# Block minima taken from PSUM, one-element reductions as moves, and rescaling on GpSimd in a fused attention and gated-MLP kernel

## The chip, the core and the metric

The kernel runs on one core of a Trainium2 chip. The metric is device time in microseconds (us) of one execution. The engines are named as in the profile: PE (TensorE matmul), PEld (its weight loads), DVE (VectorE), ACT (ScalarE), POOL (GpSimd) and SP (SyncE, which here only issues DMAs).

## What is computed

The input x is 2048 tokens by 448 features. One branch is multi-head attention with 16 heads of 28 features, the other a gated MLP with 1792 hidden features; a sigmoid gate per token mixes them. Everything is float32.

```python
q, k, v = split(x @ wqkv)                       # 16 heads, head size 28
p = softmax(einsum("bhqd,bhkd->bhqk", q, k) * 28 ** -0.5)
a = einsum("bhqk,bhkd->bhqd", p, v) @ wo
h = relu(x @ W_gate) * (x @ W_up)
b = h @ W_down
g = sigmoid((x * gate_w).sum(-1))
out = g * a + (1 - g) * b
```

## The kernel before

The schedule is written out by hand: each engine executes its instructions strictly in the order in which the program text issues them, and waits at semaphores.

**Three stages.** First the projections (q, k, v, split into high and low float32r parts), then the attention, then the down projection with the output projection. The attention goes through 32 *visits*, two for each head `h`: visit `v` handles half of the keys (8 chunks of 128) of head `v // 2` against all queries (4 blocks `j` of 512). The gate and up projections of the MLP are threaded through the visits as filling for PE (`gu_mm`, letter `x`).

**Scores.** `score()` makes a *pair*: two 128x512 matmuls into one two-bank PSUM tile from `ps_w`, then one ACT instruction over 128x1024. The softmax maximum is found in two ways. For query blocks 0 and 1 the maximum was found one head ahead by `smax` (matmuls into another `ps_w` tile, then a DVE maximum over 128x1024, L196), and travels in two additional rows of Q, so ACT takes the exponential straight from PSUM (L290). Blocks 3 and 2 are *raw* in nearly every visit (`RAW`; visit 0 has block 3 alone): ACT copies the negated score to SBUF (L292). `block_min` then takes the minimum over the four pairs of a block on DVE (L242 for the first two pairs, L244 for the third and fourth), `all_max` brings it across partitions (a transposing reduction L255, four small moves L257, L258, L260, L261, a reduction L259, a transpose L263), `take_max` subtracts it on GpSimd, 128x2048 at a time (L269), and `take_exp` takes the exponential on ACT (L276).

**PSUM.** While the visits run, `ps_w` hands out three two-bank slots strictly in turn, to scores and to `smax` alike. The matmuls of a pair therefore wait until the pair three before it has been read by whoever reads it last. The two other banks (`ps_x`) serve the gate and up projections and the products with V.

**End of a visit.** `pv` multiplies with V, in two halves (letters P and Q, 64 matmuls in all). In odd visits `rescale` brings raw blocks of the two visits to a common maximum: part 0 (letter c) subtracts two small 32x16 pieces (L611) and transposes them (L612), part 1 (letter f) takes an exponential (L615) and multiplies the 64x512 part of the output (L616), all on DVE but the exponential. `row_sums` and `spread` send the sums through DRAM, `normalise` multiplies on GpSimd (L654).

**What sets the order.** One string per kind of visit (`FIRST`, `O4`, `E3`, `O3`, `L5` to `L7`), one letter per step: s a score pair, m a `smax`, x one gate or up matmul, b a `block_min`, A an `all_max`, g a subtraction, e an exponential, c and f the rescaling, n `smax_end`, w a weight split, P and Q the products. Scores run four pairs ahead of their visit (`AHEAD = 4`). `small_things(2 * v + 1)` runs at the tenth s of a visit.

Of the kernel before, what the change touches and what calls it, by code (L numbers as in the profile page):

```python
# [8 lines left out]
F32 = mybir.dt.float32  # L9
# [9 lines left out]
P = 128  # L19
# [23 lines left out]

NP = 10

FIRST = "sbsbxbAxxxxlusgxsxsxsxxssxsesxxxsxbxbxgsxbAxxxxxxexPwQ"

O4 = "nssxxmxsxxbsxssbxbxsxxmAxsgxxgxswxxsxsxxsxxsxsecmxxmxxxxsxbxsxmxbxxxxgmxxexxebmxxxAgxmwefPQ"

E3 = "ssxmxsxxsxsxsxsbxbxbsxAxxxgxssxsgexxmxgxxmxxxsmxxsxxsmsxeexmbxxbgexmsxmPwbAQ"  # L50

O3 = "sxsxxsmssbxbbssxxxxsmsAgxxsxsxsxxsgxxmxxemxxxxsmnscxxsbbbgxmxxxxgwxxeAexexmwmPfQ"

L5 = "ssxsbsxxsxwssxxxxbxxssxxxxssxxsxxsbxxxAsxsbxxggxbxwexsxxxxcxxbgxxxegxxxxexxxxeAnPfQ"

L6 = "sssxxxsssxbxbxxxswxxxxssssxbxxxsxxxgegsAxsgxxexxxbxxxsxbxsbxxxxxxxxgAxxxxxxPeeQ"

L7 = "ssxxxxsbbswxbxxxxxxxxxxxxsxxsxxsAxsxxxxxgxsxgxexscgxexxxfxxxegxxxexsxsxPwQ"

ROUNDS = [  # L60
    (FIRST, 2), (O4, 4), (E3, 3), (O3, 3), (E3, 3), (O4, 4), (E3, 3), (O3, 3),
# [17 lines left out]
def gated_mix_kernel(ctx, tc, x, wq, wo, wgu, wd, out):  # L79
# [40 lines left out]
    def low(dst, src, high):  # L120
        nc.vector.tensor_tensor(dst, src, f32(high), op=OP.subtract)  # L121
# [36 lines left out]
    def load_k(h):  # L158
        for r in range(4):
            nc.sync.dma_start(f32(K[h % 3])[DH * r:DH * (r + 1)], qk_d[r % 2, 2 * DH * h:2 * DH * h + DH, :])  # L160
# [39 lines left out]
    def smax_end(h):  # L200

        pt = ps_x(f"mt_{h}")
        n = NU[h]
        nc.tensor.transpose(pt[:n, :P], M.pop(h), ident)
        mr = keep.tile([n, P], F32, name=f"mr_{h}", tag="mr", bufs=1)
        mh = keep.tile([n, 2, P], F32R, name=f"mh_{h}", tag="mh", bufs=1)
        nc.scalar.activation(mr, pt[:n, :P], AF.Copy)
        nc.scalar.activation(mh[:, 0], mr, AF.Copy)
        low(mh[:, 1], mr, mh[:, 0])
        for r in range(2):  # L210
            nc.sync.dma_start(f32(Q[h])[GD + r:GD + r + 1, :n * P], f32(mh)[:, r])

# [21 lines left out]
    def block_min():  # L234

        if not todo_max:
            return
        v, j, p = todo_max[0]
        if (v, j) not in R2:
            R2[v, j] = att.tile([P, 2, TB], F32, name=f"r2_{v}_{j}", tag="r2", bufs=1)  # L240
            left[v, j] = NK // 4 - 2
            nc.vector.tensor_tensor(R2[v, j], todo_max.pop(0)[2], todo_max.pop(0)[2], op=OP.min)  # L242
            return
        nc.vector.tensor_tensor(R2[v, j], R2[v, j], todo_max.pop(0)[2], op=OP.min)  # L244
        left[v, j] -= 1
        if left[v, j]:
            return
        q = NK // 8 * (v % 2)
        todo_all.append((v, j, [(v, j, q), (v, j, q + 1)]))

    def all_max():
        v, j, quads = todo_all.pop(0)
        to = ((0, 11) if j == 2 else (9, 10))[v % 2]
        a, b = (1 - v % 2, 9) if j == 2 else (1, 9 + v % 2)
        nc.vector.tensor_reduce(MN[:, 1:3], R2.pop((v, j)).rearrange("p a (b r) -> p a b r", r=32), axis=AX.X, op=OP.min,  # L255
                                apply_transpose=True)
        nc.vector.tensor_copy(MN[:64, 3:5], MN[64:, 1:3])  # L257
        nc.vector.tensor_copy(MN[:32, 5:9], MN[32:64, 1:5])  # L258
        nc.vector.tensor_reduce(MN[:32, to], MN[:32, a:b].rearrange("p a b -> p b a"), axis=AX.X, op=OP.min)  # L259
        nc.vector.tensor_copy(MN[32:64, to], MN[:32, to])  # L260
        nc.vector.tensor_copy(MN[64:, to], MN[:64, to])  # L261
        RM[v, j] = att.tile([P, TB], F32, name=f"rm_{v}_{j}", tag="rm", bufs=2)
        nc.vector.transpose(RM[v, j], MN[:, to].unsqueeze(2).to_broadcast([P, 16, 32]))  # L263
        todo_sub.extend((v, j, q) for q in quads)
# [13 lines left out]
    def score():  # L278

        v, done, q, half, chunks = stream.pop(0)  # L280
        h = v // 2
        if q not in QUAD:
            QUAD[q] = p_slot(next(slots) % NP, f"P_{v}_{q[1]}_{q[2]}")
        ps = ps_w(f"s_{v}_{chunks[0][0]}_{chunks[0][1]}")
        for c, (k, j) in enumerate(chunks):
            nc.tensor.matmul(ps[:, c], K[h % 3][:, k * P:(k + 1) * P], Q[h][:, j * TB:(j + 1) * TB], start=True, stop=True)  # L286
            AT[v, k, j] = QUAD[q][:, 2 * half + c]
        dst = QUAD[q][:, 2 * half:2 * half + 2]
        if done:
            nc.scalar.activation(dst, ps, AF.Exp, scale=SCALE)  # L290
        else:
            nc.scalar.activation(dst, ps, AF.Copy, scale=-1.0)  # L292
            todo_max.append((v, chunks[0][1], dst))

    X = {}

# [305 lines left out]
    def rescale(v, part):  # L602

        h = v // 2
        if v % 2 == 0:
            return
        rows = slice(64, P)
        if part == 0:
            RS[h] = fe.tile([P, TB], F32, name=f"rs_{h}", tag="rb", bufs=1)
            for r, a, b in ((slice(64, 96), 11, 0), (slice(96, P), 10, 9)):  # L610
                nc.vector.tensor_tensor(MN[r, 1], MN[r, a], MN[r, b], op=OP.subtract)  # L611
            nc.vector.transpose(RS[h][rows], MN[rows, 1].unsqueeze(2).to_broadcast([64, 16, 32]))  # L612
        else:
            d = RS.pop(h)[rows]
            nc.scalar.activation(d, d, AF.Exp, scale=SCALE)  # L615
            nc.vector.tensor_tensor(OS[h][rows], OS[h][rows], d, op=OP.mult)  # L616

    PO = {}

# [46 lines left out]
    def small_things(u):  # L666

        h, q = divmod(u, 4)

        if u in (16, 32):  # L670
            g = u // 16 + 1
            nc.sync.dma_start(V[:, g % 2], v_d[g])
        if u == 1:
            gates()
        if u == 2:
            pack_wo()
        if h and q == 1:
            row_sums(h - 1)
            spread(h - 1)
            if h + 2 < H:  # L680
                load_k(h + 2)
                load_q(h + 2)

    split_f(0, act_high, pool_low, (0,))
    fetch_f(1)
    for v, (order, nu) in enumerate(ROUNDS):
# [6 lines left out]
        for o in order:  # L693
            if o == "x" and not passes:
                continue
            if o == "s":
                ns += 1
                if ns == 10:
                    small_things(2 * v + 1)
                if stream:  # L700
                    score()
            elif o == "m":
                if m < len(maxima):
                    smax(m)
                    m += 1
            elif o == "x":
                i, half, n = passes.pop(0)
                if n == 0:
                    units.append((i, half, ps_x(f"gu_{i}_{half}")))
                gu_mm(units[-1][2], i, half, n)  # L710
                if n == NT - 1:
                    i, half, ps = units.pop()
                    spill_h(i, ps) if half else relu(i, ps)
                    if half:
                        finished.add(i)
                        load_f(i + 2)
            elif o == "n":
                if v % 2 and v < 2 * H - 1:
                    smax_end(v // 2 + 1)
            elif o == "w":  # L720
                ready = nxt + (ROUNDS[v + 1][1] if v + 1 < len(ROUNDS) else 2)
                ready = min(ready + ready % 2, 2 * NF)
                while parts < ready and (parts < 4 or parts // 2 - 2 in finished):
                    split_f(parts // 2, act_high, pool_low, (parts % 2,))
                    parts += 1
                    if parts % 2 == 0:
                        fetch_f(parts // 2 + 1)
            elif o == "b":
                block_min()
            elif o == "A":  # L730
                all_max()
            elif o == "g":
                take_max()
            elif o == "e":
                take_exp()
            elif o in "cf":
                rescale(v, "cf".index(o))
            elif o == "l":
                sends.pop()()
            elif o == "u":  # L740
                split_f(0, act_high, pool_low, (1,))
                QS.append(last_q("Q2"))
                for a, b in ((GD, 12), (GD + 12, 4)):
                    nc.sync.dma_start(f32(QS[2])[a:a + b].rearrange("p j t -> p (j t)"), Q[1][GD + 2:GD + 2 + b].bitcast(F32))
                load_k(2)
                load_q(2)
                fetch_f(2)
                parts = 2
            elif o in "PQ":
                if o == "P" and v and v % 2 == 0:  # L750
                    normalise(v // 2 - 1)
                pv(v, "PQ".index(o))
        rest = [k for k in todo_exp + todo_sub + todo_all if k[0] == v]
        assert not passes and not rest and v not in PO or len(stream) == max(0, 16 * (2 * H - 1 - v) - AHEAD), (v, passes, rest, len(stream) + 16 * (v + 1))
# [184 lines left out]
```

## Time and profile before

| | |
|---|---|
| time, median of 3 runs | 1548.31 us (1546.1 to 1550.45) |
| profiled execution | 1548.23 us, span 1546.5 us |
| busy over the span | PE 1280.5 us (83%), DVE 1242.8 us (80%), ACT 875.5 us (57%), POOL 765.5 us (50%) |
| granted PE clock, mean | 0.918 |

The span is the time from the first to the last instruction of the profile; 1.73 us of the execution's own time lie around it. Busy time of DVE includes what an instruction spends being held up after it has started. PE is busy while any matmul is in its pipeline. The visits occupy about 155 to 1348 us of the span.

### The profile page before, as it was taken

To read this page: it belongs to the slowest core of one execution; us is meant where nothing else is said; L and a number is where in the kernel's file an instruction comes from. 1 tells how busy PE (TensorE), PEld (TensorE's weight loads), DVE (VectorE), ACT (ScalarE), POOL (GpSimd) and SP (SyncE) were. 2 spreads that over 40 slices of the span, in tenths; PEclk is the share of its full clock that TensorE was granted. 3 is DMA by queue.
4 is the path that set the end of the run, shared out by engine and by line. 5 is a ranking of instruction groups with operands and counts; after the bars stand their busy time and mean duration, and the time that the engine had idled before them with its cause. 6 is when DMAs were issued, how large, how long until landed. Compare 5 with 4: busy or idle time off the path is not lost. (4 is left out here: it accounts for less than half of the span.)

```text
span 1546.5 us, 16880 instructions
## 1 busy us (share of the span) xinstructions
PE 1280.5 (83%) x6183; PEld 883.9 (57%) x6183; DVE 1242.8 (80%) x1242; ACT 875.5 (57%) x956; POOL 765.5 (50%) x280
## 2 busy tenths in 40 slices
PE   9998688868787868786878788877887869779999
PEld 7886455535454535454555455545555545469998
DVE  6564889998999999899889998999788996665333
ACT  5226667766766656566665656665666766421221
POOL 4223656674755454546354635464555556454110
PEclk9999889988899989999898888999999989999999
DMA  9664433341425231413251313141514122373442
GB/s 318 232 237 162 150 103 92 112 120 64 122 89 173 59 95 64 121 52 102 90 174 52 105 60 105 60 114 51 159 64 103 54 71 76 110 233 110 133 145 79
DMA packets 63807, 178.37 MB, mean 115 GB/s; under 512 B 13498, under 2 KB 20098, under 8 KB 59074
## 3 DMA queue, kind: packets, MB, share of 16 engines
q1 hardware_dynamic: 56988, 151.00, 32.4%
q0 software_dynamic: 6304, 25.82, 4.3%
q8 instruction: 49, 0.80, 0.2%
q10 hardware_dynamic: 432, 0.46, 0.1%
q14 instruction: 34, 0.28, 0.1%
HBM read 118.58 MB, written 58.87 MB: 115 GB/s over the span
## 5 line engine op out<-in xcount | busy, mean ns | idle before, releaser
L269 POOL TENSOR_TENSOR P<-P,rm 128x2048 f32<-128x2048 f32 x102 | 484.7, 4769 | 385.4 <-DVE rm L263 323.0
L286 PE MATMUL s<-Q,K 128*128 128x512 f32 x1024 | 359.0, 445 | 177.1 <-DVE mx L196 174.7
L575 PE MATMUL gu<-X,wg 128*128 128x512 f32 x1232 | 412.9, 428 | 37.1 <-DVE h L588 21.4
L196 DVE TENSOR_REDUCE mx<-sm 128x1 f32<-128x1024 f32 x256 | 307.1, 1214 | 87.2 <-PE sm L192 86.9
L286 PEld LDWEIGHTS s<-Q,K 128*128 128x128 f32 x1024 | 203.8, 211 | 272.4 <-DVE mx L196 204.6
L575 PEld LDWEIGHTS gu<-X,wg 128*128 128x128 f32 x1232 | 257.4, 209 | 107.2 <-DVE h L588 25.7
L292 ACT ACTIVATE P<-s 128x1024 f32<-128x1024 f32 x204 | 201.2, 1025 | 196.4 <-PE s L286 195.9
L290 ACT ACTIVATE P<-s 128x1024 f32<-128x1024 f32 x206 | 201.7, 1038 | 108.6 <-PE s L286 107.7
L628 PE MATMUL po<-P,V 128*32 128x512 f32 x1640 | 235.0, 602 | 5.3 <-ACT P L276 2.8
L244 DVE TENSOR_TENSOR r<-r,P 128x1024 f32<-128x1024 f32 x102 | 197.1, 1933 | 7.3
L276 ACT ACTIVATE P<-P 128x2048 f32<-128x2048 f32 x102 | 190.7, 1908 | 12.8 <-POOL P L269 12.5
L192 PE MATMUL sm<-K,Q 128*128 128x512 f32 x520 | 174.1, 419 | 21.7 <-DVE mx L196 14.2
L269 POOL TENSOR_TENSOR V<-V,rm 128x2048 f32<-128x2048 f32 x24 | 115.6, 4817 | 90.5 <-DVE rm L263 83.2
L838 PE MATMUL acc<-WD,hh 128*128 128x448 f32 x672 | 141.0, 369 | 5.3 <-POOL WD L124 3.7
L628 PE MATMUL po<-V 128*32 128x512 f32 x408 | 137.9, 605 | 8.4 <-DVE h L588 8.4
L242 DVE TENSOR_TENSOR r<-P 128x1024 f32<-128x1024 f32 x51 | 136.8, 2683 | 7.4 <-ACT P L292 6.4
L838 PEld LDWEIGHTS acc<-WD,hh 128*128 128x128 f32 x672 | 127.4, 190 | 17.3 <-POOL WD L124 4.7
L628 PEld LDWEIGHTS po<-P,V 128*32 128x32 f32 x1640 | 63.9, 111 | 126.9 <-issue 111.4
L192 PEld LDWEIGHTS sm<-K,Q 128*128 128x128 f32 x520 | 101.7, 202 | 56.0 <-DVE mx L196 25.0
L115 ACT ACTIVATE hh<-hr 128x512 fp32r<-128x512 f32 x56 | 35.2, 631 | 127.4 <-PE acc L838 121.2
L121 DVE TENSOR_TENSOR hh<-hr,hh 128x512 fp32r<-128x512 f32 x56 | 51.2, 914 | 64.8 <-ACT hh L115 64.8
L611 DVE TENSOR_TENSOR mn<-mn 32x16 f32<-32x16 f32 x32 | 89.7, 2802 | 0.7
(86 smaller groups left out, 1264.3 us busy)
## 6 DMA issues: line engine op xcount, KB each, us to landing
wg<-ws_d SPq DMA_DIRECT2D x42, 896.0 KB
K<-qk_d SPq DMA_DIRECT2D x64, 224.0 KB
Q<-qk_d SPq DMA_DIRECT2D x64, 224.0 KB
h_d<-h SPq DMA_DIRECT2D x56, 256.0 KB
hr<-h_d SPq DMA_DIRECT2D x56, 256.0 KB
ws_d<-wg SPq DMA_DIRECT2D x14, 896.0 KB
qk_d<-st POOLq DMA_DIRECT2D x21, 512.0 KB, 3.4
wgr<-wgu SPq DMA_DIRECT2D x13, 512.0 KB
```

The source lines that it names most:

```text
L192: nc.tensor.matmul(ps[:, c, :], Q[h][:, u * P:(u + 1) * P], K[h % 3][:, k0:k0 + TB], start=True, stop=True)
L196: nc.vector.tensor_reduce(to, ps, axis=AX.XY, op=OP.max)
L242: nc.vector.tensor_tensor(R2[v, j], todo_max.pop(0)[2], todo_max.pop(0)[2], op=OP.min)
L244: nc.vector.tensor_tensor(R2[v, j], R2[v, j], todo_max.pop(0)[2], op=OP.min)
L269: nc.gpsimd.tensor_tensor(QUAD[q], QUAD[q], m, op=OP.subtract)
L276: nc.scalar.activation(q, q, AF.Exp, scale=-SCALE)
L286: nc.tensor.matmul(ps[:, c], K[h % 3][:, k * P:(k + 1) * P], Q[h][:, j * TB:(j + 1) * TB], start=True, stop=True)
L290: nc.scalar.activation(dst, ps, AF.Exp, scale=SCALE)
L292: nc.scalar.activation(dst, ps, AF.Copy, scale=-1.0)
L575: nc.tensor.matmul(ps, WS[i][:, s, a], xf(i // NF, b), start=(n == 0), stop=(n == NT - 1))
L628: nc.tensor.matmul(po[32 * j:32 * j + 32], V[:, h // 4 % 2, k, h % 4], AT.pop((v, k, j)), start=(k == k0), stop=(k == k0 + NK // 2 - 1))
L838: nc.tensor.matmul(ACC[i // NF][t][:, :D], HH[i][:, a, t * P:(t + 1) * P], WD[:, f, b], start=(f == 0 and n == 0), stop=(f == NF - 1 and n ...
```

## The change

1. In all visits but the first, `block_min` reads the newer score pair where the matmuls left it, in PSUM. It does so with a `scalar_tensor_tensor` (times -1, then minimum) whose other input is in SBUF: the negated first pair, or the running minimum. ACT still copies each raw pair to SBUF, since GpSimd works on that copy. The minimum now also holds the PSUM slot. The instruction waits for ACT's copy of the same pair.
2. The four small moves in `all_max` become `tensor_reduce` over an axis of one element.
3. Both small subtractions and the multiplication of `rescale` move from DVE to GpSimd. DVE keeps the transpose between them, which now waits for GpSimd.
4. `smax_end` reads its transposed maxima from PSUM twice, without the copy to SBUF in between (L207).
5. `normalise` gets a letter of its own, N, early in the odd visits; it stood at P of the even visits before. `small_things` comes at the sixth s; the loads of the next K and Q, which were part of it, stay at the tenth.
6. All seven order strings are written anew.

```diff
-O4 = "nssxxmxsxxbsxssbxbxsxxmAxsgxxgxswxxsxsxxsxxsxsxsecmxxmxxxxsxbxsxmxbxxxxgmxxexxebmxxxAgxmwefPQ"
...
+O4 = "ssbnxxNxxsxxxbsxbxxxsAgwxxsxgxxsssxxsxsxxxxmxexxmmxsxexgxmxxxmxsxsxmgxxmxexmsbxxsbxxscefbxPwAQ"
...
-        mr = keep.tile([n, P], F32, name=f"mr_{h}", tag="mr", bufs=1)
...
-        nc.scalar.activation(mr, pt[:n, :P], AF.Copy)
-        nc.scalar.activation(mh[:, 0], mr, AF.Copy)
-        low(mh[:, 1], mr, mh[:, 0])
+        nc.scalar.activation(mh[:, 0], pt[:n, :P], AF.Copy)
+        low(mh[:, 1], pt[:n, :P], mh[:, 0])
...
-        v, j, p = todo_max[0]
+        v, j, x, _ = todo_max.pop(0)
         if (v, j) not in R2:
-            R2[v, j] = att.tile([P, 2, TB], F32, name=f"r2_{v}_{j}", tag="r2", bufs=1)
-            left[v, j] = NK // 4 - 2
-            nc.vector.tensor_tensor(R2[v, j], todo_max.pop(0)[2], todo_max.pop(0)[2], op=OP.min)
-            return
-        nc.vector.tensor_tensor(R2[v, j], R2[v, j], todo_max.pop(0)[2], op=OP.min)
+            r = att.tile([P, 2, TB], F32, name=f"r2_{v}_{j}", tag="r2", bufs=1)
+            left[v, j] = NK // 4 - 1
+            before, (_, _, x, ps) = x, todo_max.pop(0)
+        else:
+            r = before = R2[v, j]
+            ps = _
+        R2[v, j] = r
+        if ps is None:
+            nc.vector.tensor_tensor(r, x, before, op=OP.min)
+        else:
+            nc.vector.scalar_tensor_tensor(r, ps, -1.0, before, op0=OP.mult, op1=OP.min)
         left[v, j] -= 1
...
+    def move(dst, src):
+
+        nc.vector.tensor_reduce(dst, src.unsqueeze(len(src.shape)), axis=AX.X, op=OP.min)
...
-        nc.vector.tensor_copy(MN[:64, 3:5], MN[64:, 1:3])
-        nc.vector.tensor_copy(MN[:32, 5:9], MN[32:64, 1:5])
+        move(MN[:64, 3:5], MN[64:, 1:3])
+        move(MN[:32, 5:9], MN[32:64, 1:5])
...
-        nc.vector.tensor_copy(MN[32:64, to], MN[:32, to])
-        nc.vector.tensor_copy(MN[64:, to], MN[:64, to])
+        move(MN[32:64, to], MN[:32, to])
+        move(MN[64:, to], MN[:64, to])
...
-            todo_max.append((v, chunks[0][1], dst))
+            todo_max.append((v, chunks[0][1], dst, ps if v else None))
...
-                nc.vector.tensor_tensor(MN[r, 1], MN[r, a], MN[r, b], op=OP.subtract)
+                nc.gpsimd.tensor_tensor(MN[r, 1], MN[r, a], MN[r, b], op=OP.subtract)
...
-            nc.vector.tensor_tensor(OS[h][rows], OS[h][rows], d, op=OP.mult)
+            nc.gpsimd.tensor_tensor(OS[h][rows], OS[h][rows], d, op=OP.mult)
...
-                if ns == 10:
+                if ns == 6:
                     small_things(2 * v + 1)
+                if ns == 10 and v % 2 == 0:
+                    loads(v // 2)
...
+            elif o == "N":
+                if v > 1 and v % 2:
+                    normalise(v // 2 - 1)
...
-                if o == "P" and v and v % 2 == 0:
-                    normalise(v // 2 - 1)
```

DVE in visit 19, around its rescaling, before. `h` is the hidden tile of the MLP, `mn` the small tile of minima, `rs` the rescaling factors, `mx` the maxima from a `smax` pair `sm`, `r` the running minimum and `P` a copied score in SBUF:

```order
L588 TENSOR_TENSOR h_5929<-gu_1_5874,rl_5800 128x512
L611 TENSOR_TENSOR mn<-mn 32x16 x2
L612 STREAM_TRANSPOSE rs_5983<-mn 64x512
L196 TENSOR_REDUCE mx_5877<-sm_5987 128x1
L196 TENSOR_REDUCE mx_5877<-sm_5994 128x1
L242 TENSOR_TENSOR r_20_3_6008<-P_3_0_5970 128x1024
L196 TENSOR_REDUCE mx_5877<-sm_6016 128x1
L244 TENSOR_TENSOR r_20_3_6008<-r_20_3_6008,P_3_1_6002 128x1024
```

The same engine and visit now (`s` is a score pair in PSUM):

```order
L196 TENSOR_REDUCE mx_5932<-sm_5999 128x1
L196 TENSOR_REDUCE mx_5932<-sm_6006 128x1
L248 SCALAR_TENSOR_TENSOR r_20_3_6014<-s_2_3_6010,P_3_0_5986 128x1024
L248 SCALAR_TENSOR_TENSOR r_20_3_6014<-s_4_3_6019,r_20_3_6014 128x1024
L620 STREAM_TRANSPOSE rs_6030<-mn 64x512
L248 SCALAR_TENSOR_TENSOR r_20_3_6014<-s_6_3_6026,r_20_3_6014 128x1024
L263 TENSOR_REDUCE mn<-r_20_3_6014 128x32
```

The subtractions have left DVE, the transpose has moved behind the first minima of the next visit's block 3, and those minima read `s`.

GpSimd over the same visit, before: the last two subtractions of visit 19 and the first two of visit 20 (`rm` is the maximum spread over partitions):

```order
L269 TENSOR_TENSOR P_2_2_5865<-P_2_2_5865,rm_2_5926 128x2048
L269 TENSOR_TENSOR V<-V,rm_2_5926 128x2048
L269 TENSOR_TENSOR P_3_0_5970<-P_3_0_5970,rm_3_6058 128x2048
L269 TENSOR_TENSOR P_3_1_6002<-P_3_1_6002,rm_3_6058 128x2048
```

and now the four subtractions of visit 19 and the first of visit 20, with the normalisation of the head before ahead of them:

```order
L662 TENSOR_TENSOR os_5340<-os_5340,rb_5645 128x512
L277 TENSOR_TENSOR P_3_2_5747<-P_3_2_5747,rm_3_5811 128x2048
L277 TENSOR_TENSOR P_3_3_5771<-P_3_3_5771,rm_3_5811 128x2048
L277 TENSOR_TENSOR P_2_2_5831<-P_2_2_5831,rm_2_5892 128x2048
L277 TENSOR_TENSOR V<-V,rm_2_5892 128x2048
L619 TENSOR_TENSOR mn<-mn 32x16 x2
L624 TENSOR_TENSOR os_5829<-os_5829,rs_6030 64x512
L277 TENSOR_TENSOR P_3_0_5986<-P_3_0_5986,rm_3_6064 128x2048
```

The rescaling stands between the last subtraction of one visit and the first of the next.

PE at the first raw pairs of visit 20, before (`gu` is the gate or up projection, `s_20_4_3` the pair of visit 20, key chunk 4, block 3):

```order
L286 MATMUL s_20_4_3_6003<-Q1_106,K1_103 128x512 x2
L575 MATMUL gu_32_1_5991<-X0_111,wg_32_5741 128x512 x2
L286 MATMUL s_20_6_3_6011<-Q1_106,K1_103 128x512 x2
L575 MATMUL gu_32_1_5991<-X1_112,wg_32_5741 128x512
L192 MATMUL sm_184_6016<-K2_104,Q2_1188 128x512 x2
```

and now:

```order
L192 MATMUL sm_187_6006<-K2_104,Q2_1185 128x512 x2
L294 MATMUL s_20_2_3_6010<-Q1_106,K1_103 128x512 x2
L583 MATMUL gu_33_0_5984<-X0_111,wg_33_5880 128x512 x2
L294 MATMUL s_20_4_3_6019<-Q1_106,K1_103 128x512 x2
L583 MATMUL gu_33_0_5984<-X1_112,wg_33_5880 128x512
L583 MATMUL gu_33_0_5984<-X0_111,wg_33_5880 128x512
L294 MATMUL s_20_6_3_6026<-Q1_106,K1_103 128x512 x2
L583 MATMUL gu_33_0_5984<-X1_112,wg_33_5880 128x512
```

The `smax` pairs no longer stand between these raw pairs; one or two gate or up matmuls do, and the products with V of visit 19 follow directly.

More of the change, by code (lines that the diff above doesn't have):

```diff
@@ L44 @@
 NP = 10
[L46 to L58, printed above, removed]
+FIRST = "sbsbxbAxxxlusssxxsxgsxxxxxsssxbgxexssbxxbxxxxexPwAQ"
+O4 = "ssbnxxNxxsxxxbsxbxxxsAgwxxsxgxxsssxxsxxxxmxexxmmxsxexgxmxxxmxsxsxmgxxmxexmsbxxsbxxscefbxPwAQ"
+E3 = "gsmsxbxsxbxsxxbxsxxxxsxxssxxAssxmexxmxxsxxxxmsxmgxxmexgsmxgxxmxessexsbPwbbAQ"
+O3 = "sgsxxbxxsxxxsxxbbsxxgxxAssgsxxxgsmsxmxexmxNsmnwxsmsxsmseexxbxxxxxbxxsxmexmbPcfAwQ"
+L5 = "ssNbnsxxxgxxxsxxsxbbxxsxxexxxxxsAxsxgxssxgxxsxxsxgxxxsxxsswbxxxxxwexxexexsbxcfxxPbAQ"
+L6 = "gssxsxsxxxxxbxsbxxxsbexsxxxxsxxAxxxsxsxxxsgxsxesxxsgxxbxxxxexxsgxxwxxbsbxxAxePQ"
+L7 = "gssxxgbsxwbsxxxxxsxxxexsxxbxxAsxxsxxxxxxxxxxxsxsggxxxxxxxeeexxsNxcxxxfsxwPQ"
 ROUNDS = [
@@ L679, in small_things, with loads @@
             spread(h - 1)
-            if h + 2 < H:
-                load_k(h + 2)
-                load_q(h + 2)
+    def loads(h):
+        if 2 < h + 2 < H:
+            load_k(h + 2)
+            load_q(h + 2)
     split_f(0, act_high, pool_low, (0,))
```

## The prediction

> **What bounds the kernel now.** I first cut the span into the three stages (busy time of each engine by stretch; the columns after the length are PE, PEld, DVE, ACT and POOL with instruction counts, then the granted PE clock).
>
> ```profile
> core 0: us, PE busy (x) PEld busy (x) DVE busy (x) ACT busy (x) POOL busy (x), PEclk, DMA share, GB/s
> 0.00:155.00 155.00, 148.13 (x638) 119.32 (x642) 88.50 (x110) 63.54 (x118) 50.89 (x66) 0.98 0.67 237
> 155.00:1348.00 1193.00, 945.82 (x4664) 595.43 (x4657) 1066.50 (x1025) 768.18 (x773) 663.03 (x179) 0.90 0.32 95
> 1348.00:1546.00 198.00, 186.51 (x891) 169.17 (x889) 87.83 (x109) 43.75 (x66) 51.60 (x36) 0.98 0.46 141
> ```
>
> Before and after the visits PE is busy 96% and 94% of the time, and the change hardly touches these stages. In the visits, 1193 us or 37.3 us each, PE has the larger page share, yet DVE is the fuller engine: 1066.5 of 1193 is 89%, PE 79%. The list of waits says who waits for whom:
>
> ```profile
> POOL P L269 <- DVE rm L263: 323.0, 40, 16.1
> ...
> PE s L286 <- DVE mx L196: 174.7, 48, 7.9
> ...
> PE sm L192 <- DVE mx L196: 14.2, 15, 3.3
> ```
>
> PE's largest idle time, 174.7 + 14.2 = 189 us, is waiting for a maximum on DVE to give back a PSUM slot; GpSimd too waits mostly for DVE. In the visits PE idles 1193 - 945.8 = 247 us, so 58 us have other causes.
>
> Is DVE busy with work? The views of single lines give minimum, median and maximum duration in ns:
>
> ```profile
> L242 DVE TENSOR_TENSOR r<-P x51: 1182/2964/5262, 135.5 to 1314.8; 128x1024 f32<-128x1024 f32 x51
> L244 DVE TENSOR_TENSOR r<-r,P x102: 1214/1226/5475, 136.8 to 1323.5; 128x1024 f32<-128x1024 f32 x102
> L611 DVE TENSOR_TENSOR mn<-mn x32: 166/4152/4503, 186.9 to 1332.8; 32x16 f32<-32x16 f32 x32
> L616 DVE TENSOR_TENSOR os<-os,rs x16: 689/3538/5049, 208.9 to 1338.8; 64x512 f32<-64x512 f32 x16
> L588 DVE TENSOR_TENSOR h<-gu,rl x56: 650/676/693, 164.2 to 1358.7; 128x512 f32<-128x512 f32 x56
> L196 DVE TENSOR_REDUCE mx<-sm x256: 1159/1216/1227, 54.2 to 1238.9; 128x1 f32<-128x1024 f32 x128
> L269 POOL TENSOR_TENSOR P<-P,rm x102: 4492/4612/5632, 146.7 to 1332.7; 128x2048 f32<-128x2048 f32 x102
> ```
>
> The first four take two tensors from SBUF, and all four stretch: a 32x16 subtraction that can be done in 166 ns typically takes 4152, about one GpSimd subtraction (4612). The next two, which have a PSUM input and at most one from SBUF, never stretch (693 and 1227 at most). So much of DVE's busy time is being held up by GpSimd.
>
> **The change, term by term.** DVE in the visits, for the lines L242, L244, L611, L616 and L121 in this order (us, count):
>
> ```profile
> 155.00:1348.00 1193.00, 166.47 (x62) 0.90 0.32 95
> 155.00:1348.00 1193.00, 242.03 (x124) 0.90 0.32 95
> 155.00:1348.00 1193.00, 89.68 (x32) 0.90 0.32 95
> 155.00:1348.00 1193.00, 52.57 (x16) 0.90 0.32 95
> 155.00:1348.00 1193.00, 16.64 (x15) 0.90 0.32 95
> ```
>
> *Minima.* 62 + 124 = 186 instructions, 408.5 us, become as many with one PSUM and one SBUF input. The trace has this operation in another shape:
>
> ```profile
> L844 DVE SCALAR_TENSOR_TENSOR y<-acc,gate,ga x16: 676/679/684, 1417.2 to 1542.8; 128x448 f32<-128x448 f32 x16
> ```
>
> Scaled by elements, 679 x 1024/448 = 1.55 us is the upper end; the 1.216 us maximum over the same 1024 elements (L196) is the lower. I take 1.28, nearer to L196: from L588 (512 elements, 676 ns) to L244's minimum (1024, 1214 ns) an element more costs 1.05 ns, and 679 + 576 x 1.05 = 1284 ns. 186 x 1.28 = 238 us: DVE saves 170 (bounds 120 to 182).
>
> *Rescaling.* DVE loses 89.7 + 52.6 = 142 us. GpSimd gets 32 small subtractions and 16 of 64x512; its nearest rows:
>
> ```profile
> L654 POOL TENSOR_TENSOR os<-os,rb x15: 1317/2215/2290, 234.5 to 1303.9; 128x512 f32<-128x512 f32 x15
> L124 POOL TENSOR_TENSOR wg<-wgr,wg x39: 721/1010/1995, 158.6 to 430.1; 128x384 fp32r<-128x384 f32 x26, 64x256 fp32r<-64x256 f32 x13
> ```
>
> Between nothing and 721 ns for a small one I take 0.3 (16 elements against 256 and more), and 2.0 for the others (1.3 to 2.3): 10 + 32 = 42 us, 663 + 42 = 705 on GpSimd, 22 us per visit, below PE's work. DVE's transpose now waits for GpSimd, with minima, `all_max` and hidden tiles queued behind it, and PE waits for those: see the first rival. The multiplication releases the addition to the second half's output, after 64 matmuls that PE does meanwhile.
>
> *Maxima transposed* (L121's 15):
>
> ```profile
> L121 DVE TENSOR_TENSOR mh<-mr,mh x16: 235/238/4472, 99.1 to 1277.7; 8x128 fp32r<-8x128 f32 x15, 12x128 fp32r<-12x128 f32 x1
> ```
>
> With one PSUM input instead of two SBUF inputs I take the median for all, 15 x 0.24 = 3.6 us instead of 16.6, saving 13. ACT loses 16 copies, some 4 us, hidden.
>
> *Moves.* 63 x 4, off and on in equal number:
>
> ```profile
> L257 DVE COPY mn<-mn x63: 175/177/592, 141.2 to 1326.0; 64x32 f32<-64x32 f32 x63
> L198 DVE TENSOR_REDUCE m<-mx 128x8 f32<-128x16 f32 x16 | 2.7, 170 | 0.6
> ```
>
> A reduction of 16 elements takes 170 ns, a copy 177: nothing, between -5 and +5 us. The copies hardly ever stretch here, because GpSimd is waiting for their result. The Trainium skill, SBUF — State Buffer, section "Who interferes with whom", says that a copy in a two-port mode is blocked for the whole of a GpSimd instruction, while `tensor_reduce` never contends on trn2. By that rule the moves would pay once GpSimd has work at this place, as the rescaling could give it, 16 times up to 2 us; but that would be a loss avoided, and the sum stays the same.
>
> *Normalisation, earlier small things, loads.* Same instructions, same engine. On SP's queue the loads of K stood behind the wait of `spread`:
>
> ```profile
> 924.46 0.41 SPq L644 DMA_DIRECT2D l_d<-rq  x1
> 929.09 1.71 SPq L650 DMA_DIRECT2D rb<-l_d  x4
> 930.84 1.68 SPq L160 DMA_DIRECT2D K<-qk_d  x4
> ```
>
> The 4.6 us hole moves four pairs ahead; the loads keep their place, a visit before use. Hidden; uncovered it would cost 16 x 4.6 = 74 us.
>
> *DVE's sum:* 1066 - 170 - 142 - 13 = 741 us, 23.2 per visit. It stops being the bound, so the saving is not 325 us: PE is late next.
>
> *PE's work.* Matmuls in the visits, for L286, L575, L192 and L628 (PE busy and count first):
>
> ```profile
> 155.00:1348.00 1193.00, 345.00 (x984) 195.50 (x984) 0.90 0.32 95
> 155.00:1348.00 1193.00, 395.56 (x1169) 245.39 (x1170) 0.90 0.32 95
> 155.00:1348.00 1193.00, 151.60 (x448) 88.11 (x448) 0.90 0.32 95
> 155.00:1348.00 1193.00, 234.72 (x2048) 66.81 (x2040) 0.90 0.32 95
> ```
>
> These overlap, so I price them by spacing, from the line's durations and the timeline around 900 us:
>
> ```profile
> L628 PE MATMUL po<-P,V x1640: 592/592/1062, 154.4 to 1346.9; 128*32 128x512 f32 x183
> ```
>
> ```profile
> 903.00 2.73 PE L628 MATMUL po<-P,V 128*32 128x512 f32 x20
> ...
> 909.71 0.39 PE L575 MATMUL gu<-X,wg 128*128 128x512 f32 x1
> ...
> 911.16 0.63 PE L575 MATMUL gu<-X,wg 128*128 128x512 f32 x2
> ...
> 916.30 1.33 PE L575 MATMUL gu<-X,wg 128*128 128x512 f32 x5
> ...
> 923.60 0.50 PE L575 MATMUL gu<-X,wg 128*128 128x512 f32 x1 [1.81 <-DVE h L588]
> ...
> 925.41 1.04 PE L575 MATMUL gu<-X,wg 128*128 128x512 f32 x2
> ```
>
> Five take 1.33, one 0.39: (1.33 - 0.39)/4 = 0.235 us each. Twenty of the products with V, in fives of four, take 2.73: less 0.59 for the last, 0.107 each. Then 2601 x 0.235 + 2048 x 0.107 = 611 + 219 = 830 us. PE is busy 946: 116 us more, since the clock falls after idle time. Soon after the wait of 1.81 us two matmuls take 1.04, where they took 0.63. So each us of idle time costs 116/247 = 0.47 us more.
>
> *The sum.* The stage is 830 + 1.47 x idle time (before: 830 + 1.47 x 247 = 1193). Should the 189 us of waits go entirely, 58 stay: 915. If waits went by DVE's free share, which rises from 11% to 741 of about 1000, that is 26% free, 41% of them would stay. I take 30%, since the new order spreads matmuls between the pairs; half is my upper bound, because minima now hold slots. 30% is 57: idle 115, stage 830 + 169 = 999. Outside the visits 353.5, around the span 1.7: **1354 us** (0%: 1270; half: 153 idle, 1410). The profiled execution's 1548.2 stands for the median of 1548.3.
>
> **The rivals.**
>
> *First: DVE stuck at GpSimd's queue.* The transpose of the rescaling waits behind a 4.61 us subtraction and two small ones, about 5.4 us in each of 16 heads, 87 us that PE sees in full. Idle 58 + 57 + 87 = 202, stage 1127, 1482 us. For it: GpSimd's last subtraction of a visit stands directly ahead. Against it: PE has the products with V there, some 6.8 us (64 x 0.107).
>
> *Second, slower: the slots become a serial ring.* Each of the 186 pairs is now released after ACT's copy,
>
> ```profile
> L292 ACT ACTIVATE P<-s x204: 997/1026/1104, 120.1 to 1315.6; 128x1024 f32<-128x1024 f32 x102
> ```
>
> and after the minimum, 1.03 + 1.28 us instead of 1.03. Were PE to wait out each minimum: idle 58 + 186 x 1.28 = 296, stage 1265, 1620 us. It decides from 189/186 = 1.02 us of wait for each minimum upward. For it: slots come strictly in turn, and a minimum behind an `all_max` is late. Against it: between slots stand gate and up matmuls, and DVE's queue is a third shorter. The Trainium skill, PSUM — Partial Sum Buffer, section "Terms", forbids two engines in one bank at once, reads included, so copy and minimum cannot overlap; no run here shows that, and by it the hold is the whole 2.3 us, as reckoned.
>
> *Third: the stretching stays.* If it hung on something other than the second SBUF input, the new minima would stretch as well, and the time stays at 1548. L588 and L196 speak against it.
>
> **Numbers.** Forecast 0.70 (1265 to 1410), first rival 0.16 (1410 to 1543), third 0.02, second 0.12. The range 1265 to 1465 holds the forecast and most of the first rival, about 8 in 10. Faster by over 0.3% 0.86, within 0.3% (about what a measurement can tell) 0.02, slower 0.12.
>
> **What would show it.** Right: minima at 1.2 to 1.4 us with no long tail; DVE near 740 us and PE busy near 885 in the visits; clock above 0.9; GpSimd's rows still near 4.6. Wrong: PE waiting over 1 us per minimum (second rival), a wait of DVE's transpose for GpSimd of some 5 us (first), or minima stretched to 3 us (third).

## The result, and the profile after

The changed kernel takes 1240.4 us (median of 4, 1239.6 to 1244.6) against 1549.4 us: ratio 0.801, interval 0.799 to 0.804. The direction was forecast; the size was not. The forecast of 1354 us gave a range from 1265 us, and 1240 lies below it, below even the 1270 us that I reckoned with no wait for maxima left.

Busy time by stage after the change (columns as before; the visits now end near 1042 us):

```profile
0.00:155.00 155.00, 148.28 (x642) 118.09 (x646) 89.00 (x114) 63.87 (x118) 50.66 (x66) 0.99 0.66 236
155.00:1042.00 887.00, 874.32 (x4667) 534.38 (x4660) 734.06 (x973) 757.07 (x757) 653.70 (x227) 1.00 0.43 128
1042.00:1239.00 197.00, 185.99 (x884) 168.91 (x882) 87.62 (x108) 44.01 (x66) 51.56 (x36) 0.97 0.47 144
```

The outer stages are as they were. The visits fell from 1193 to 887 us: PE is busy 874 of them (98.6%), idle 13 instead of 247, and its granted clock reads 1.00 instead of 0.90. DVE went from 1066 to 734 us, as forecast (741). The kernel is now bound by PE.

The single lines that carried the argument (minimum, median and maximum in ns), the new minima, the small moves, GpSimd's subtraction and the maxima transposed:

```profile
L248 DVE SCALAR_TENSOR_TENSOR r<-s,r x124: 1212/1225/1227, 154.8 to 1020.2; 128x1024 f32<-128x1024 f32 x124
L248 DVE SCALAR_TENSOR_TENSOR r<-s,P x50: 1211/1224/1226, 152.1 to 1017.6; 128x1024 f32<-128x1024 f32 x50
L257 DVE TENSOR_REDUCE mn<-mn x252: 158/172/209, 141.5 to 1023.9; 64x32 f32<-64x32 f32 x63, 32x16 f32<-32x16 f32 x63
L277 POOL TENSOR_TENSOR P<-P,rm x102: 4572/4635/4686, 147.0 to 1029.6; 128x2048 f32<-128x2048 f32 x102
L121 DVE TENSOR_TENSOR mh<-mt,mh x16: 258/269/272, 99.4 to 964.0; 8x128 fp32r<-8x128 f32 x15, 12x128 fp32r<-12x128 f32 x1
```

No minimum that reads PSUM stretches any more. By the start times in the trace, 120 of the 186 begin while a GpSimd instruction runs, and none takes longer than 1227 ns. The list of waits has lost the large entries of PE, whose longest single wait in the visits is now 3.3 us, for ACT. These are the entries that matter for the rivals (the first two are waits of the weight loads, PEld; the matmuls themselves wait 0.4 us for a minimum):

```profile
PEld s L294 <- DVE r L248: 15.6, 40, 0.8
PEld s L294 <- DVE mx L196: 12.9, 35, 0.7
...
DVE rs L620 <- POOL mn L619: 12.6, 2, 10.6
```

### The profile page after: what moved, and what is told of

Same layout as the page of the kernel before. It is cut to its first block, busy times and chain, and to the rows that moved or that the text cites. A ratio compares the mean times of both kernels' runs of the same rounds, so it can differ in the third digit from the quotient of the medians.

```text
span 1239.1 us, 16877 instructions
## 1 busy us (share of the span) xinstructions
PE 1208.6 (98%) x6183; PEld 821.4 (66%) x6183; DVE 910.7 (73%) x1194; ACT 865.0 (70%) x940; POOL 755.9 (61%) x328
## 4 chain that ended last, share of the span: by engine, by line
PE 72%; DVE 9%; ACT 7%; DMA 6%; issue 4%; POOL 2%; SPq 1%; DVEq 0%; POOLq 0%; ACTq 0%
PE po L636 16%; PE gu L583 14%; PE s L294 13%; PE acc L852 10%; PE sm L192 8%; PE qk L415 5%; DVE r L248 4%; DVE mx L196 3%; PE wo L811 3%; PE v L433 3%; ACT P L300 2%; DMA X<-x_d 2%; ACT P L298 1%; ACT P L284 1%; DMA l_d<-rq 1%
## 5 line engine op out<-in xcount | busy, mean ns | idle before, releaser
L277 POOL TENSOR_TENSOR P<-P,rm 128x2048 f32<-128x2048 f32 x102 | 470.3, 4634 | 118.8 <-DVE rm L271 116.8
L583 PE MATMUL gu<-X,wg 128*128 128x512 f32 x1232 | 375.1, 398 | 8.3 <-ACT os L642 3.3
L294 PE MATMUL s<-Q,K 128*128 128x512 f32 x1024 | 322.8, 411 | 5.5 <-ACT P L298 1.7
L583 PEld LDWEIGHTS gu<-X,wg 128*128 128x128 f32 x1232 | 231.4, 189 | 69.8 <-DMA X<-x_d 6.5
L294 PEld LDWEIGHTS s<-Q,K 128*128 128x128 f32 x1024 | 178.5, 189 | 106.6 <-DVE r L248 15.6
L248 DVE SCALAR_TENSOR_TENSOR r<-s,r 128x1024 f32<-128x1024 f32 x124 | 151.8, 1224 | 34.6 <-ACT P L300 19.8
L192 PE MATMUL sm<-K,Q 128*128 128x512 f32 x520 | 165.8, 403 | 2.5 <-DVE mx L196 2.4
L192 PEld LDWEIGHTS sm<-K,Q 128*128 128x128 f32 x520 | 91.5, 188 | 40.2 <-ACT P L298 11.7
L248 DVE SCALAR_TENSOR_TENSOR r<-s,P 128x1024 f32<-128x1024 f32 x50 | 61.2, 1223 | 48.7 <-ACT P L300 48.6
L263 DVE TRANSPOSE_TENSOR_REDUCE mn<-r 128x32 f32<-128x1024 f32 x63 | 77.6, 1232 | 1.3
```

The costliest lines, as they stand in the source:

```text
L192: nc.tensor.matmul(ps[:, c, :], Q[h][:, u * P:(u + 1) * P], K[h % 3][:, k0:k0 + TB], start=True, stop=True)
L248: nc.vector.scalar_tensor_tensor(r, ps, -1.0, before, op0=OP.mult, op1=OP.min)
L277: nc.gpsimd.tensor_tensor(QUAD[q], QUAD[q], m, op=OP.subtract)
L583: nc.tensor.matmul(ps, WS[i][:, s, a], xf(i // NF, b), start=(n == 0), stop=(n == NT - 1))
```

## The experiments

Two theories stood at the start. A: DVE was held up by GpSimd wherever it takes two SBUF inputs, and the hold-ups set the time. B: the new orders spread the pairs so that TensorE stops waiting, whatever DVE does. The first four kernels undo parts of the change; the later ones ask how DVE's load becomes waiting on PE.

**Only the new orders** (e1_orders_only). The changed kernel with all its operations put back:

```diff
-            todo_max.append((v, chunks[0][1], dst, ps if v else None))
+            todo_max.append((v, chunks[0][1], dst, None))
...
-        nc.vector.tensor_reduce(dst, src.unsqueeze(len(src.shape)), axis=AX.X, op=OP.min)
+        nc.vector.tensor_copy(dst, src)
...
-                nc.gpsimd.tensor_tensor(MN[r, 1], MN[r, a], MN[r, b], op=OP.subtract)
+                nc.vector.tensor_tensor(MN[r, 1], MN[r, a], MN[r, b], op=OP.subtract)
```

(likewise the multiplication of `rescale`, and `smax_end`).

> The changed kernel with only its order strings, the letter N and the sixth s kept: minima from SBUF, copies as moves, rescaling on VectorE, maxima copied first. Theory A (VectorE was held up by GpSimd wherever it takes two SBUF inputs, and that set the time): the hold-ups come back, VectorE about 1060 us busy in the visits, 1480 to 1600 us. Theory B (the new orders spread the pairs so that TensorE stops waiting, whatever VectorE does): most of the gain stays, below 1400 us.

Measured: 1516.9 us, ratio 0.979 (0.978 to 0.981). The orders alone give 32 us of the 309. Theory B falls, in so far as the orders without the new operations gain little; all the new operations in the old order were not run, so how far they need the new order stays open. (The letter N stands early in ten of its fifteen visits only; in the order `O3` it is in the middle, in `L7` near the end.) The groups of this kernel (us, mean ns) show that the orders move the hold-ups rather than end them:

```profile
L121 DVE TENSOR_TENSOR mh<-mr,mh 8x128 fp32r<-8x128 f32 x15 | 62.8, 4185 | 0.0
...
L621 DVE TENSOR_TENSOR mn<-mn 32x16 f32<-32x16 f32 x32 | 13.8, 430 | 0.4
```

The small subtractions of the rescaling take 0.43 us instead of 2.80: 30 of the 32 start while GpSimd is idle and take 0.17 us, where before 26 of the 32 started while it ran. But the low part of the transposed maxima takes 4.2 us instead of 1.1.

**Minima from SBUF** (e2_min_sbuf): the first edit of the diff above, alone.

> The changed kernel with the minima taken from the SBUF copies as before. Theory A: 186 minima at 2 to 2.3 us instead of 1.22, VectorE at 734 + 145 to 200 = about 900 us in the visits, more than the 887 us that they take now, so 1330 to 1450 us. Theory B: under 1290 us.

Measured: 1472.4 us. Reading PSUM is worth 232 us in the new order, the largest part by far, and more than I expected of theory A. DVE has 971 us in the visits, 237 more, and the minima stretch again:

```profile
L246 DVE TENSOR_TENSOR r<-P,r x102: 1204/1226/5475, 137.4 to 1246.2; 128x1024 f32<-128x1024 f32 x102
L246 DVE TENSOR_TENSOR r<-P x51: 1204/2254/5575, 136.2 to 1237.2; 128x1024 f32<-128x1024 f32 x51
```

By their start times, the 108 that begin while GpSimd is idle take 1.20 to 1.23 us, and the 81 that begin while it runs 4.17 us on the average.

**Rescaling back on DVE** (e3_rescale_dve): both `gpsimd` in `rescale` become `vector`.

> The changed kernel with both steps of the rescaling back on VectorE. Theory A: the 32 small subtractions take 2 to 4 us again and the 16 multiplications about 3 us, VectorE at 734 + 100 to 140 = about 860 us of 887: TensorE starts to wait, 1260 to 1340 us. Theory B: under 1260 us.

Measured: 1250.1 us, 10 more, which is what I had written down for theory B and not for A. Hold-ups are rare here:

```profile
L619 DVE TENSOR_TENSOR mn<-mn x32: 166/171/4554, 190.3 to 1038.1; 32x16 f32<-32x16 f32 x32
L624 DVE TENSOR_TENSOR os<-os,rs x16: 689/689/691, 192.1 to 1046.1; 64x512 f32<-64x512 f32 x16
```

29 of the 32 small subtractions start while GpSimd is idle. So the new order itself removed these hold-ups; moving the work to GpSimd adds little. This fits theory A as well, since GpSimd is idle at that place; the run alone doesn't decide between the two.

**Copies as moves** (e4_copies): the second edit of the diff above, alone.

> The changed kernel with copies as moves. By the rows of before (172 ns against 177 ns, GpSimd waiting for the result): 1240 us within 5. If copies are held up by GpSimd's rescaling beside them: up to 16 times 1.3 us more on VectorE, still within 10 us.

Measured: 1295.1 us, 55 more; a clear miss. One of the four copies carries it, the first one (group, us and mean ns), and the timelines of DVE and of GpSimd show one case:

```profile
L257 DVE COPY mn<-mn 64x32 f32<-64x32 f32 x63 | 78.8, 1250 | 2.2
```

```profile
656.17 2.55 DVE L248 SCALAR_TENSOR_TENSOR r<-s,r 128x1024 f32<-128x1024 f32 x2
658.75 1.25 DVE L263 TRANSPOSE_TENSOR_REDUCE mn<-r 128x32 f32<-128x1024 f32 x1
660.03 3.31 DVE L257 COPY mn<-mn 64x32 f32<-64x32 f32 x2
663.38 0.40 DVE L267 TENSOR_REDUCE mn<-mn 32x16 f32<-32x144 f32 x1
```

```profile
653.88 4.62 POOL L277 TENSOR_TENSOR V<-V,rm 128x2048 f32<-128x2048 f32 x1 [7.94 <-DVE rm L271]
658.46 4.63 POOL L277 TENSOR_TENSOR P<-P,rm 128x2048 f32<-128x2048 f32 x1
```

Block 2's chain reaches its first copy while GpSimd is still subtracting block 3's maximum; the copy lasts until that instruction ends (658.46 + 4.63 = 663.09, then the second copy). Before the change DVE mostly arrived there when GpSimd was done: 5 of the 63 first copies began while it ran, against 40 of 63 here. In the changed kernel 40 of the 63 first moves begin while GpSimd runs too, and as reductions they take 0.18 us.

**More work on DVE, without hold-ups.** A useless reduction after each transposing reduction of `all_max`, so inside the chain from the last minimum to the spread maximum (e5_work_in_chain), or behind the chain (e6_work_after_chain):

```diff
+        nc.vector.tensor_reduce(SPARE, r2, axis=AX.XY, op=OP.min)
```

> The changed kernel with a useless reduction over 128x1024 on VectorE (1.2 us, one SBUF input) after the transposing reduction of each block's maximum, so 63 x 1.2 = 77 us more work inside the chain from the last minimum to the spread maximum. Chain theory (what is late next is the way from the minima to GpSimd's subtraction): 1290 to 1320 us, as with the held-up copies. Load theory (VectorE has 887 - 734 = 153 us free in the visits, only its sum counts): the same time as the next kernel within 15 us.

> The same useless reduction, but after the maximum has been spread, so the same 77 us of load outside the chain. Chain theory: under 1265 us. Load theory: the same time as with the work inside the chain.

Measured: 1265.9 and 1263.4 us, the same within their spread. So the place within the chain doesn't matter, and 60 us more on DVE cost 23 to 26 us. The held-up copies had cost twice that for 71 us more.

**Each minimum twice** (e7_min_twice): the `scalar_tensor_tensor` is issued a second time with `r` as its other input.

> The changed kernel with each minimum from PSUM done twice: 186 x 1.22 = 228 us more on VectorE, 962 us in the visits, about what the minima from SBUF made of it, but as work and with the PSUM slots held longer. If sums decide, VectorE is the bound at nearly 100%: 1320 to 1400 us. If the queue behind VectorE decides as it did with the minima from SBUF (1472 us): 1440 to 1500 us. If the slots become a serial ring: over 1500 us.

Measured: 1415.3 us, between my cases, and DVE 954 of 1062 us in the visits. The PSUM slots are held 1.2 us longer, and no serial ring forms: PE's waits for the second minimum are its longest entry now, but 63 us in all, 0.34 us for each of 186. For 17 us more on DVE the minima from SBUF took 57 us more: nearly the same load, without the longer hold on the slots, but in pieces of up to 5.5 us.

**Half of GpSimd's subtraction** in the kernel before (e8_half_sub); the other half of each subtraction is left out:

```diff
-        nc.gpsimd.tensor_tensor(QUAD[q], QUAD[q], m, op=OP.subtract)
+        nc.gpsimd.tensor_tensor(QUAD[q][:, :2], QUAD[q][:, :2], m[:, :2], op=OP.subtract)
```

> The kernel before, with GpSimd's subtraction of the maximum done for half of the elements only (the other half of the scores stays as it is), 2.3 us instead of 4.6. Theory A (VectorE instructions with two SBUF inputs wait for GpSimd's running one): the hold-ups become half as long and rarer, the mean of the first minimum falls from 2.66 to about 1.6 us, that of the small subtractions from 2.8 to about 1.2 us; VectorE saves about 200 us, 1330 to 1420 us. Rival (the stretching has another cause): 1530 to 1550 us.

Measured: 1334.0 us. No DVE instruction was touched, yet the small subtractions of the rescaling and the first minima shrink with GpSimd's instruction, the former's median from 4152 to 1969 ns:

```profile
L611 DVE TENSOR_TENSOR mn<-mn x32: 167/1969/2360, 181.8 to 1117.7; 32x16 f32<-32x16 f32 x32
L242 DVE TENSOR_TENSOR r<-P x51: 1205/1225/3012, 135.8 to 1107.9; 128x1024 f32<-128x1024 f32 x51
L269 POOL TENSOR_TENSOR P<-P,rm x102: 2340/2410/3407, 147.0 to 1117.6; 128x1024 f32<-128x1024 f32 x102
```

That GpSimd's running instruction is the cause of the stretching is shown by this, and by the start times in the kernel before: the 26 small subtractions that begin while GpSimd runs take 0.86 to 4.50 us, the 6 others 0.17 us. How much of the 215 us comes from shorter hold-ups, and how much from GpSimd's own earlier end, this run doesn't separate.

**The same useless work in lumps** (e9_lumps): three reductions in a row at every third block.

```diff
+        for _ in range(0 if (2 * v + j) % 3 else 3):
+            nc.vector.tensor_reduce(SPARE, r2, axis=AX.XY, op=OP.min)
```

> The changed kernel with the useless reduction after the spread maximum, three in a row at every third block (21 x 3.7 us) instead of one at each: the same 77 us, in lumps as long as a held-up copy. If the size of one delay decides (the held-up copies cost 55 us for about 70 us of VectorE, the evenly spread reductions 23 for 62): 1285 to 1310 us. If only the sum decides: 1258 to 1270 us, and the copies then cost more for another reason.

Measured: 1307.3 us, 67 more than the changed kernel, where the same work spread evenly cost 23. Here PE waits again for slots that DVE has to read (waits in the visits):

```profile
PE s L297 <- DVE mx L196: 19.4, 10, 2.9
PE sm L192 <- DVE mx L196: 14.4, 7, 5.1
PE s L297 <- DVE r L248: 13.1, 6, 3.2
```

These are 47 us; the same three entries of the even work (e6) are 3.1, 7.5 and 1.0, 12 us. Between these two kernels, how long DVE is away at one time decides, and not how much it does.

**Transposed maxima through SBUF** (e10_mh_sbuf): `smax_end` as before.

> The changed kernel with the transposed maxima copied to SBUF first and their low part taken from there, as before. With the new orders alone these 15 subtractions took 4.2 us each instead of 0.27. If that repeats, 59 us more on VectorE in lumps of 4 us: 1265 to 1300 us. By the sum that was forecast for this edit (13 us of VectorE, hidden): 1240 to 1250 us.

Measured: 1277.3 us, 37 more, for 34 us more on DVE. The 15 subtractions all begin while GpSimd runs, and take 2.6 us on the average, less than the 4.2 us that I expected from e1.

**Rescaling on GpSimd alone**, in the kernel before (e11_rescale_pool_alone).

> The kernel before, with the rescaling alone on GpSimd. VectorE loses 142 us of 1066 in the visits. By the slope of the runs so far (about 0.7 us of TensorE idle time for each us of VectorE, and the clock's loss with it) 1400 to 1450 us. If VectorE now waits at its transpose behind GpSimd's subtractions (the first rival of the prediction): 1500 to 1570 us.

Measured: 1492.4 us; a gain of 56 us, less than the slope promised. DVE fell by 81 us only, since hold-ups came back elsewhere: the minima of the third and fourth pairs (L244, from copies in `P`) have a mean of 2275 ns now, 1933 before, and all minima together take 64 us more. DVE's transpose never waits for GpSimd here.

**Minima of one block from SBUF**: of block 2 (e12_min_half) and of block 3 (e13_min_block3_sbuf).

```diff
-            todo_max.append((v, chunks[0][1], dst, ps if v else None))
+            todo_max.append((v, chunks[0][1], dst, ps if v and chunks[0][1] == 3 else None))
```

> The changed kernel with the minima of block 3 from PSUM and those of block 2 from SBUF. If the hold-ups of the two blocks are alike, half of the 237 us that all minima from SBUF gave to VectorE: about 850 us in the visits, TensorE idle about 80 us, 1320 to 1370 us. If a threshold decides (VectorE full or not): under 1300 us.

> The mirror of the kernel before it: the minima of block 2 from PSUM, those of block 3 from SBUF. If the hold-ups fall on block 2 alone (its minima meet GpSimd's two subtractions of block 3; block 3's are taken while GpSimd has nothing ready), 93 minima at 1.22 to 1.4 us: 1238 to 1260 us, perhaps a little under the changed kernel, since block 3's slots come free sooner. If both blocks are held up when they read SBUF: 1320 to 1470 us.

Measured: 1469.1 and 1253.7 us. Block 2 alone costs as much as both (1472), block 3 only 13 us. My first expectation, that both are alike, was wrong; for e13 I expected block 2 to carry the hold-ups, and it does. The minima of e12 and e13, from SBUF:

```profile
L246 DVE TENSOR_TENSOR r<-P,r x52: 1224/3654/5479, 137.2 to 1247.1; 128x1024 f32<-128x1024 f32 x52
L246 DVE TENSOR_TENSOR r<-P x26: 1205/4018/5570, 135.9 to 1239.7; 128x1024 f32<-128x1024 f32 x26
```

```profile
L246 DVE TENSOR_TENSOR r<-P,r x52: 1207/1225/2136, 136.9 to 1021.0; 128x1024 f32<-128x1024 f32 x52
L246 DVE TENSOR_TENSOR r<-P x26: 1204/1226/5540, 135.7 to 1016.4; 128x1024 f32<-128x1024 f32 x26
```

and the timelines of DVE and GpSimd in e12:

```profile
710.51 2.81 DVE L246 TENSOR_TENSOR r<-P 128x1024 f32<-128x1024 f32 x1 [0.34 <-ACT P L300]
713.43 6.79 DVE L246 TENSOR_TENSOR r<-P,r 128x1024 f32<-128x1024 f32 x2
```

```profile
707.63 10.18 POOL L277 TENSOR_TENSOR P<-P,rm 128x2048 f32<-128x2048 f32 x2 [2.15 <-DVE rm L271]
```

GpSimd's two subtractions of block 3 run from 707.63 to 717.81, and three minima of block 2, 3.7 us of work, take from 710.51 to 720.22. Here the first ends at 713.32, soon after the first subtraction, and the other two are done 2.4 us after the second: about one minimum gets through between two subtractions. Block 3's minima come at the end of the visit before, mostly when GpSimd has nothing ready: of the minima that read SBUF, 23 of 96 begin while GpSimd runs in e13, and 66 of 96 in e12.

**All kernels, visits only.** PE idle is the stretch less PE's busy time.

| kernel | visits us | DVE busy us | PE idle us | PE clock | time us |
|---|---|---|---|---|---|
| changed | 887 | 734 | 13 | 1.00 | 1240 |
| rescaling on DVE (e3) | 895 | 757 | 20 | 1.00 | 1250 |
| block 3 from SBUF (e13) | 896 | 755 | 19 | 0.99 | 1254 |
| even work (e6) | 907 | 796 | 27 | 1.00 | 1263 |
| work in the chain (e5) | 909 | 794 | 28 | 0.99 | 1266 |
| maxima through SBUF (e10) | 920 | 768 | 37 | 0.99 | 1277 |
| copies (e4) | 939 | 805 | 49 | 0.98 | 1295 |
| work in lumps (e9) | 955 | 805 | 55 | 0.97 | 1307 |
| half subtraction (e8) | 976 | 841 | 86 | 0.96 | 1334 |
| minima twice (e7) | 1062 | 954 | 127 | 0.94 | 1415 |
| block 2 from SBUF (e12) | 1113 | 952 | 171 | 0.91 | 1469 |
| minima from SBUF (e2) | 1112 | 971 | 171 | 0.91 | 1472 |
| rescaling on GpSimd, before (e11) | 1136 | 986 | 197 | 0.90 | 1492 |
| orders only (e1) | 1163 | 1025 | 219 | 0.90 | 1517 |
| before | 1193 | 1066 | 247 | 0.90 | 1549 |

None of them beats the changed kernel.

## Why the prediction was right or wrong

**Right: what bound the kernel, and DVE's sum.** DVE was the bound, through hold-ups by GpSimd (e2, e8). The minima were put at 1.28 us and take 1.22, GpSimd's additions at 42 us (L619 and L624 take 7.0 + 20.6 = 28), DVE's sum at 741 us (734). The third rival is gone with the minima's maximum of 1227 ns.

**Wrong: the step from DVE's sum to PE's waits.** Three terms, with what they measured: PE's work 830 us (874 at a clock of 1.00, so 44 more), idle time 115 us (13, so 102 less), the clock's loss 54 us (none to be seen). 999 + 44 - 102 - 54 = 887. In the idle time two steps failed. I took 30% of the 189 us of waits for maxima to stay, by DVE's free share; next to nothing stayed, though DVE is still 83% busy. And I left the 58 us "of other causes" in place. They were DVE's too, in part by the list of waits of before, which I didn't add up:

```profile
PE gu L575 <- DVE h L588: 21.4, 10, 4.4
...
PE po L628 <- DVE h L588: 8.4, 1, 8.4
...
PE mt L204 <- DVE h L588: 3.1, 1, 3.1
```

These are 33 of the 58. What the free share misses is the size of one delay: e6 and e9 put nearly the same load on DVE, and PE idles 27 us with even pieces and 55 with lumps; the difference lies in PE's waits for slots. Before, most of DVE's excess lay in long pieces: 54 instructions that took 3 to 5 us longer than the shortest of their kind hold 214 of its some 340 us. That the three PSUM slots and the matmuls between them cover pieces of 1.2 us and not of 4 would explain it; no run varied the number of slots, so this mechanism is not shown. Nor is length the whole account: in e4 39 of the 54 copies that were held up lost less than 2 us, and the same load on DVE as in e9 cost 55 us against 67.

The factor 0.47 for the clock was too high as well: it put all of PE's excess over 830 us on the clock. From the changed kernel to the one before, PE's busy time rises from 874 to 946 while idle time rises by 234: 0.31 us for each. 44 us of what I gave to the clock is PE's own time.

**Wrong: the moves.** Forecast -5 to +5 us; in the changed kernel they are worth 55. The rows of before showed copies that hardly stretch, and I let them speak for the kernel after. The rule of the Trainium skill (SBUF — State Buffer, "Who interferes with whom") held: a copy in a two-port mode waits out GpSimd's instruction (up to 4266 ns in e4), a `tensor_reduce` does not (209 ns at most here). I thought of GpSimd's rescaling as what could come beside them; what came was block 3's subtraction, since DVE now reaches block 2's chain sooner.

**Wrong: what the rescaling is worth.** I gave it 142 us of DVE. Undone in the changed kernel it costs 10, alone in the old one it gains 56. Likewise the transposed maxima: 13 us of DVE, hidden, by the forecast; 37 us of time when undone. A hold-up needs both an instruction that can be held up and GpSimd running at its place in the order, so shares from one order don't carry over to another. Undone one at a time, the parts cost 232 + 55 + 37 + 10 = 334 us, more than the 277 us that undoing all four costs (1517 - 1240): one hold-up hides another.

**The rivals.** First: DVE's transpose did wait for GpSimd, but twice in 16, 12.6 us in all, where I had 87. Second: minima keep the weight loads of pairs waiting 15.6 us in all, 0.08 us for each of 186, where the ring decides from 1.02. Third: gone, as said.

## What to carry to other kernels

A busy share near 90% on an engine whose like instructions range from 0.17 to 4.2 us can be a sign of being held up rather than of work: compare minimum and median line by line, and look at what the other engine runs at that moment. When the hold-ups go, take away all waits that hang on that engine's queue, those under other names too, and look at the length of single delays as well as at the engine's free share when you price what stays. An instruction that doesn't stretch in the old schedule may do so in the new one, when something beside it moves: so protect the whole chain, as the moves do here.

## What the runs showed of the hardware

- A minimum over 128x1024 float32 with one input in PSUM and one in SBUF takes 1.22 us, the same as with both in SBUF when GpSimd is idle (1.20 to 1.23 in e2).
- A 64x32 copy of 0.18 us lasts up to 4.27 us beside a GpSimd subtraction (e4's L257 view: 164/177/4266 ns); the same move as a one-element reduction never exceeds 0.21 us.
- GpSimd seems to be held up as well, but little: its subtraction has a maximum of 5632 ns before and 4686 ns after the change, at medians of 4612 and 4635, and with the minima from SBUF (e2) GpSimd is busy 704 us in the visits instead of 654.
- In the stretch of e12 shown, DVE's minima from SBUF get through one at a time between GpSimd's instructions, so that a row of three loses more than one GpSimd instruction.
- PE's mean granted clock over the visits falls as its idle share rises: 1.00 with 1.4% idle, 0.97 with 6%, 0.94 with 12%, 0.90 with 17 to 21%.
